# Early attention of a fused attention and two-layer MoE kernel: mask products ahead of the scores on TensorE, and VectorE's second scan ahead of the mask

## The chip, the cores and the metric

One core of a Trainium2 chip runs the whole program. The metric is the device time of one execution in microseconds; lower is better. The engines are TensorE (PE, matrix products into the eight PSUM banks), VectorE (DVE), ScalarE (ACT), GpSimd (POOL) and SyncE (SP, whose queue starts the transfers).

## The reference, cut to what matters

A gated linear attention over 4 batches, 8 heads, 768 steps and a head width of 48, then two feed-forward layers over the 3072 tokens.

```
for t in range(S):
    state = alpha[:, :, t, :, None] * state + einsum('bhd,bhe->bhde', k[:, :, t], v[:, :, t])
    y[:, :, t] = einsum('bhd,bhde->bhe', q[:, :, t], state)
x = y.transpose(0, 2, 1, 3).reshape(B * S, H * D)          # 3072 x 384
h = x @ w_in;  x1 = (h * sigmoid(h)) @ w_out               # 384 -> 2048 -> 384
g = x1 @ w_gate;  out = (g * sigmoid(g) * (x1 @ w_val)) @ w_out2   # 384 -> 1536 -> 384
```

## The kernel before

The steps are cut into 6 chunks of 128 for each of the 4 batches: 24 chunks, `n = 0..23`. A chunk has 4 pairs of heads; a pair of one chunk is a group `g = 4n..4n+3` (96 groups), and two groups make a duo `d`. For each group TensorE makes the scores (`qkt`, tile `s`: a product of the scaled keys and queries `kq` for each of the two heads, and one with a unit matrix that turns the keys). VectorE multiplies the scores with the causal mask (`causal`, tile `pt`), and ScalarE copies the turned keys (`keys`, tile `kt`). ScalarE's copy reads the same bank as VectorE's product and waits for it. When all four groups of a chunk are there, TensorE makes the chunk's results (`pv`: `y`, the state's increment `ds`, and from the fifth chunk on the part from the state that is carried), and `chunk_end` splits `y` into a high and a low half for the next layer (ScalarE copies, VectorE subtracts, tile `x`; in the second block of tokens a tile `y` too).

What the scores need is made by two scans on VectorE for each duo: `stage_a1` (a scan backwards, tile `r`; then `stage_a2`, a reciprocal and on POOL the scaled keys) and `stage_a3` (a scan forwards, tile `g`, and on POOL the scaled queries; after a chunk's second duo it issues the load of the chunk after next, tile `in`).

All order is that of the program text. One call of `attn` handles one group: it issues `pv` of a finished chunk where there is one, then `qkt` of the new group, then on VectorE and ScalarE the mask and the keys, then `chunk_end`, then the scans that are due. The first 7 chunks (28 groups) are "early": nothing but attention runs, with 32-bit scores in two banks that are used in turn, so that group g+2 waits for the readers of group g. `pv(m)` runs in the call of group 4m+5. From group 16 on (`T0 = first - 12`) the calls also decode weights: `units1` takes one unit (a 128 by 384 part of the first layer's weights; there are 32) through three steps on VectorE (tiles `raw`, `dec`), a rounding on ScalarE and a subtraction on POOL (tile `w`).

After the early part the first layer's products (`g1`, `g2`, tiles `h` and `x`) of the first two blocks of tokens run in turns with nothing from attention but with the rest of the 32 units being decoded, a unit or so per half step; then the remaining chunks' attention is mixed with the first layer, and the second layer (`gv`, `og`) ends the program. `act1` makes from a tile `h` the activation twice on ScalarE, rounded (`gh`) and in full (`gf`, one buffer in SBUF), and VectorE's subtraction of the two is the low half `gl`.

Of the kernel before, what the change touches and what calls it, by code (L numbers as in the profile page):

```python
# [10 lines left out]
F32 = mybir.dt.float32  # L11
# [3 lines left out]
AF = mybir.ActivationFunctionType  # L15
# [6 lines left out]
C = 128  # L22
NC = S // C
NCH = B * NC
NP = H // 2
# [195 lines left out]
def fast(ctx, tc, pk, w1, w2, out, bad_i):  # L221
# [3 lines left out]
    PE, ACT, DVE, POOL, SP = nc.tensor, nc.scalar, nc.vector, nc.gpsimd, nc.sync  # L225

    blocks1, n = [], 0
# [15 lines left out]
    mp = ctx.enter_context(tc.tile_pool(name="mp", bufs=2))  # L243

    def bank(i, name):
        pool = ps if i in (2, 3, 6, 7) else pools_ps["late"]
        return pool.tile([128, 512], F32, tag=f"b{i}", name=name)

    def big(i, name, dtype=F32):

        return mp.tile([128, 6 * 512], dtype, tag=f"big{i}", name=name, bufs=1)
# [8 lines left out]
    def sub(eng, lo, src, hi):  # L260
        eng.tensor_tensor(out=lo, in0=src, in1=hi.bitcast(F32), op=ALU.subtract)  # L261

    def split(hi, lo, src, lo_eng):
        ACT.activation(out=hi, in_=src, func=AF.Copy)  # L264
        sub(lo_eng, lo, src, hi)
# [8 lines left out]
    mask = ac.tile([128, C], BF16, name="mask")  # L274
# [7 lines left out]
    start = big(0, "start")  # L282
# [6 lines left out]
    y_t, ds_t, s_t = {}, {}, {}  # L289
    x_t, y3_t, p0_t = {}, {}, {}  # L290

    NE, NF = B, len(blocks1[0]) + len(blocks1[1])
# [107 lines left out]
    def columns(t):  # L400
        return t.rearrange("p (h x) -> p h x", h=2)[:, :, :D]

    def qkt(g):

        d, i = divmod(g, 2)
        n, p = divmod(g, NP)
        kf, qf = kq_t[d][:, 0, i], kq_t[d][:, 1, i]
        if n < NF:

            b = pools_ps["early"].tile([128, 2, 512], F32, tag=f"s{g % 2}", name=f"s{g}")  # L410
            for h in range(2):
                r = slice(64 * h, 64 * h + 64)
                PE.matmul(b[:, h, :C], kf[r], qf[r], start=True, stop=True)
            PE.matmul(b[:, 0, C:C + 2 * D], kf, columns(ident), start=True, stop=True)
            s_t[g] = b[:, :, :C], b[:, 0, C:C + 2 * D]
            return
        b = bank(5, f"s{g}")
        w = 2 * C + (2 * D if n < NCH - B else 0)
        kh, kl = kh_t[d][:, i], kl_t[d][:, i]
        PE.matmul(b[:, :w], kh, qh[:, p, :w], start=True, stop=False)  # L420
        PE.matmul(b[:, :2 * C], kh, ql[:, p], start=False, stop=False)
        PE.matmul(b[:, :w], kl, qh[:, p, :w], start=False, stop=True)
        s_t[g] = b[:, :2 * C].rearrange("p (h t) -> p h t", h=2), b[:, 2 * C:]

    def causal(g):
        if g < NE * NP and g % NP == 0:
            pt = p0[g // NP % 2]
        else:
            pt = ap.tile([128, 2, C], F32, tag="pt", name=f"pt{g}", bufs=NP + 1)
        pt_t[g] = pt  # L430
        DVE.tensor_tensor(
            out=pt, in0=s_t[g][0],
            in1=mask.rearrange("p (o t) -> p o t", o=1).to_broadcast([128, 2, C]), op=ALU.mult,
        )
# [10 lines left out]
    def pv(n):  # L445

        c, b = divmod(n, B)
        v = v_t[n]  # L450
        early = (NF - 1 - n) % 2 if n < NF else 0
        y = y_t[n] = bank((6, 2)[early], f"y{n}")
        first, last = n * NP, n * NP + NP
        heads = [(p, h, slice(64 * h, 64 * h + 64)) for p in range(NP) for h in range(2)]
        pts = [pt_t.pop(g) for g in range(first, last)]
        for p, h, hs in heads:
            if n < NE and p == 0:
                continue
            cs = slice(p * C, p * C + C)
            PE.matmul(  # L460
                y[hs, cs], v[:, p, hs], pts[p][:, h], start=(p == (n < NE)),
                stop=(n >= NE and c == 0 and p == NP - 1),
            )
            if n < NE:
                PE.matmul(
                    y[hs, cs], v3[n % 2][:, p - 1, hs], pts[0][:, h], start=False,
                    stop=(p == NP - 1),
                )
        if c < NC - 1:
            ds = ds_t[n] = bank((7, 3)[early], f"ds{n}")[:, :NP * D].rearrange(  # L470
                "p (r e) -> p r e", r=NP
            )
            for p, h, hs in heads:
                PE.matmul(  # L474
                    ds[hs, p], kt_t[first + p][:, hs], v[:, p, 64 * h:64 * h + D],
                    start=True, stop=True,
                )
            for g in range(first, last):
                kt_t.pop(g)
        if c:  # L480
            for p, h, hs in heads:
                PE.matmul(  # L482
                    y[64 * h:64 * h + D, p * C:p * C + C], state[b][hs, p],
                    kq_t[(first + p) // 2][hs, 1, p % 2], start=False, stop=(p == NP - 1),
                )
# [105 lines left out]
    def act1(j, f):  # L591
        w = len(blocks1[j]) * C
        hb = h_t.pop((j, f))
        gh = mp.tile([128, 512], F32R, tag="gh", name=f"gh{j}_{f}")[:, :w]
        gf = mp.tile([128, 512], F32, tag="gf", name=f"gf{j}_{f}", bufs=1)[:, :w]
        gl = mp.tile([128, 512], F32R, tag="gl", name=f"gl{j}_{f}")[:, :w]
        ACT.activation(out=gh, in_=hb, func=AF.Silu)  # L597
        ACT.activation(out=gf, in_=hb, func=AF.Silu)  # L598
        act_t[j, f] = (gh, gl)

        def rest():
            sub(DVE, gl, gf, gh)

        return rest

# [54 lines left out]
    def act2(j, f):  # L660
        w = len(blocks2[j]) * C
        gate, val = gv_t.pop((j, f))
        p = pools2["s"]
        sg = mp.tile([128, 512], F32, tag="gf", name=f"sg{j}_{f}", bufs=1)[:, :w]
        ACT.activation(out=sg, in_=gate, func=AF.Silu)  # L665
        a = p.tile([128, 512], F32, tag="a", name=f"a{j}_{f}")[:, :w]
        DVE.tensor_tensor(out=a, in0=val, in1=sg, op=ALU.mult)  # L667
        ah = mp.tile([128, 512], F32R, tag="gh", name=f"ah{j}_{f}")[:, :w]
        al = mp.tile([128, 512], F32R, tag="gl", name=f"al{j}_{f}")[:, :w]
        split(ah, al, a, DVE)  # L670
        a_t[j, f] = (ah, al)
# [26 lines left out]
    st = dict.fromkeys(("a1", "a2", "a3", "b", "c", "gd", "qk", "pv", "end", "l1", "d1", "e1", "f1", "h1", "s1", "l2", "d2", "e2", "f2", "h2", "s2"), 0)  # L698

    def up_to(key, g, fn, top=NG):  # L700
        while st[key] < min(g + 1, top):
            fn(st[key])
            st[key] += 1
# [8 lines left out]
    def attn(lag=1, more=True, first=None):  # L712
        done, new = st["pv"], None
        if st["qk"] - st["pv"] * NP >= NP + lag - 1:
            pv(done)
            st["pv"] += 1
        if more and st["qk"] < NG:
            new = st["qk"]
            qkt(new)
            st["qk"] += 1  # L720
        rest = first and first()
        if new is not None:
            d, odd = divmod(new, 2)
            early = new < NF * NP
            ahead, top = d + (2 if early else 3), NF * NP // 2 if early else ND
            if early and new and not odd:
                up_to("a1", ahead, stage_a1, top)
            causal(new)
            keys(new)
            if new == 0:  # L730
                up_to("a1", ahead, stage_a1, top)
        if rest:
            rest()
        if st["pv"] > done:
            chunk_end(done)
        if new is None:
            return
        if new < NE * NP and new % NP == NP - 1:
            spread(new // NP)
        if odd:  # L740
            up_to("a3", ahead, stage_a3, top)
            if not early:
                up_to("b", d + 2, stage_b, ND)
            up_to("gd", d, guard, ND)
        else:
            up_to("a1", ahead, stage_a1, top)
            if not early:
                up_to("c", d + 1, stage_c, ND)
            up_to("a2", ahead, stage_a2, top)
# [61 lines left out]
    for _ in range(12):  # L811
# [4 lines left out]
        out=mask, in_=mask, compare_op=ALU.is_ge, fill=0.0, base=0,  # L816
# [11 lines left out]
    first = NF * NP  # L828
# [4 lines left out]
    for i in range(NP):  # L833
        ACT.activation(
            out=qh[:, i, 2 * C:].rearrange("p (h d) -> p h d", h=2), in_=columns(ident), func=AF.Copy
        )
    T0 = first - 12
    for g in range(first):
        attn(2)
        if g % 4 == 3:  # L840
            up_to("l1", g // 4 + 1, load1, NU1)
        if g >= T0:
            units1(2, 1 + (g - T0) // 2)
    pe_stack.close()
# [12 lines left out]
    due, n = [first] * (2 * len(turns)), first  # L857
# [188 lines left out]
```

## Time and profile before

| | us |
|---|---|
| median of 3 runs | 1023.23 (1023.1 to 1025.08) |
| profiled execution: its time | 1025.6 |
| profiled execution: its span | 1023.9 |
| early part: first scores to the first product of the layer | 6.88 to 79.95 |
| TensorE busy over the span | 989.5 (97%) |
| VectorE, ScalarE, POOL busy | 476.0, 360.7, 222.8 |

The profiled execution took 1025.6 us, of which 1.7 us lie outside the span that the trace covers. Busy time of TensorE says little here: a product counts as busy from its start to its modelled end, at either level of its clock. The granted clock is given as a share of 2.4 GHz, so 0.5 is the lower level (1.2 GHz).

### The profile page before, as it was taken

The numbers are of one execution on the slowest core, as the hardware profiler recorded it, in microseconds if no ns is written. First come the engines' busy times: TensorE is split into PE (matmuls) and PEld (weight loads), VectorE is DVE, ScalarE is ACT, GpSimd is POOL, SyncE is SP. The second block draws the span as 40 slices with busy tenths as digits, with TensorE's granted clock in tenths as the row PEclk, the third lists the DMA queues.
The fourth block names the chain that finished last, engine by engine and source line by source line (L and its number), as shares of the span: only waits on it lengthen the run. The fifth ranks groups of instructions, "written<-read, shape, count | busy, mean of one in ns | idle before, by whom it ended". The sixth has DMA issues, their size and how long they took to land.

```text
span 1023.9 us, 14306 instructions
## 1 busy us (share of the span) xinstructions
PE 989.5 (97%) x5618; PEld 872.0 (85%) x5618; DVE 476.0 (46%) x847; ACT 360.7 (35%) x856; POOL 222.8 (22%) x293
## 2 busy tenths in 40 slices
PE   7868999999999999999999999999999999999997
PEld 5756998789999999988888888888888888888886
DVE  6475997545435355353498756222222222222222
ACT  2233444545545455444354323222222222222121
POOL 5351434624323244131144212000000000000000
PEclk7677999999999999999999999999999999999999
DMA  5434421222121222200454520100100100100000
GB/s 185 169 127 139 181 78 47 90 72 85 54 65 53 76 84 74 80 21 1 134 175 139 170 62 16 62 1 1 62 1 1 61 1 1 62 1 8 24 1 34
DMA packets 28458, 69.08 MB, mean 67 GB/s; under 512 B 3168, under 2 KB 9824, under 8 KB 28384
## 3 DMA queue, kind: packets, MB, share of 16 engines
q1 hardware_dynamic: 28096, 67.84, 20.6%
q8 instruction: 46, 0.75, 0.3%
q10 hardware_dynamic: 288, 0.26, 0.1%
q14 instruction: 28, 0.23, 0.1%
HBM read 56.68 MB, written 9.44 MB: 65 GB/s over the span
## 4 chain that ended last, share of the span: by engine, by line
PE 91%; DVE 4%; ACT 2%; DMA 1%; issue 1%; SPq 0%; ACTq 0%; DVEq 0%
PE gv L580 10%; PE gv L579 10%; PE gv L582 10%; PE h L579 7%; PE h L580 6%; PE h L582 6%; PE x L615 6%; PE x L614 6%; PE x L617 6%; PE o L684 5%; PE o L682 5%; PE o L683 5%; PE y L460 3%; PE y L482 2%; PE ds L474 1%; PE s L420 1%
## 5 line engine op out<-in xcount | busy, mean ns | idle before, releaser
L580 PE MATMUL gv<-x1h,w 128*128 128x512 f32 x432 | 169.1, 391 | 0.0
L579 PE MATMUL gv<-x1h,w 128*128 128x512 f32 x432 | 169.0, 391 | 0.0
L667 DVE TENSOR_TENSOR a<-gv,sg 128x512 f32<-128x512 f32 x72 | 49.8, 692 | 253.9 <-PE gv L582 253.9
L579 PE MATMUL h<-x,w 128*128 128x384 f32 (+1 forms) x336 | 124.0, 369 | 5.3 <-ACT kt L440 3.4
L614 PE MATMUL x<-gh,w 128*128 128x384 f32 (+1 forms) x336 | 122.4, 364 | 0.1
L615 PE MATMUL x<-gh,w 128*128 128x384 f32 (+1 forms) x336 | 122.3, 364 | 0.0
L582 PE MATMUL gv<-x1l,w 128*128 128x512 f32 x432 | 122.1, 391 | 0.0
L580 PE MATMUL h<-x,w 128*128 128x384 f32 (+1 forms) x336 | 121.8, 362 | 0.0
L261 DVE TENSOR_TENSOR gl<-gf,gh 128x384 fp32r<-128x384 f32 (+1 forms) x112 | 73.4, 655 | 84.3 <-ACT gf L598 82.6
L261 POOL TENSOR_TENSOR w<-raw,w 128x384 fp32r<-128x384 f32 x64 | 75.0, 1172 | 162.7 <-ACT w L556 159.9
L597 ACT ACTIVATE gh<-h 128x384 fp32r<-128x384 f32 (+1 forms) x112 | 60.0, 535 | 136.5 <-PE h L582 136.5
L665 ACT ACTIVATE sg<-gv 128x512 f32<-128x512 f32 x72 | 43.1, 599 | 177.4 <-PE gv L582 177.4
L264 ACT ACTIVATE ah<-a 128x512 fp32r<-128x512 f32 x72 | 45.6, 633 | 157.8 <-DVE a L667 157.8
L684 PE MATMUL o<-w,al 128*128 128x384 f32 x288 | 97.2, 338 | 0.0
L682 PE MATMUL o<-w,ah 128*128 128x384 f32 x288 | 97.0, 337 | 0.0
L683 PE MATMUL o<-w,ah 128*128 128x384 f32 x288 | 96.7, 336 | 0.0
L582 PEld LDWEIGHTS gv<-x1l,w 128*128 128x128 f32 x432 | 81.1, 188 | 17.8
L579 PEld LDWEIGHTS gv<-x1h,w 128*128 128x128 f32 x432 | 81.0, 188 | 15.3
L580 PEld LDWEIGHTS gv<-x1h,w 128*128 128x128 f32 x432 | 81.1, 188 | 14.9
L582 PE MATMUL h<-x,w 128*128 128x384 f32 (+1 forms) x336 | 85.4, 362 | 0.0
L617 PE MATMUL x<-gl,w 128*128 128x384 f32 (+1 forms) x336 | 84.6, 359 | 0.2 <-DVE gl L261 0.2
L579 PEld LDWEIGHTS h<-x,w 128*128 128x128 f32 x336 | 63.4, 189 | 15.4 <-issue 6.2
(104 smaller groups left out, 1572.5 us busy)
## 6 DMA issues: line engine op xcount, KB each, us to landing
raw<-in_w_dram SPq DMA_DIRECT2D x64, 384.0 KB, 3.6
in<-in_pk_dram SPq DMA_DIRECT2D x22, 770.5 KB, 4.2
in_v<-in_pk_dram SPq DMA_DIRECT2D x24, 256.0 KB, 3.1
x1r<-x_d SPq DMA_DIRECT2D x6, 768.0 KB, 5.0
out_dram<-ob SPq DMA_DIRECT2D x24, 192.0 KB, 2.1
x_d<-x1e SPq DMA_DIRECT2D x4, 576.0 KB, 3.3
x_d<-x1e SPq DMA_DIRECT2D x3, 768.0 KB, 4.6
late<-in_w_dram SPq DMA_DIRECT2D x4, 384.0 KB, 5.3
```

The costliest lines, as they stand in the source:

```text
L261: eng.tensor_tensor(out=lo, in0=src, in1=hi.bitcast(F32), op=ALU.subtract)
L579: PE.matmul(acc, part(u, k), xh, start=(k == 0), stop=False)
L580: PE.matmul(acc, part(u, k, 1), xh, start=False, stop=False)
L582: PE.matmul(acc, part(u, k), xl, start=False, stop=(k == len(xk) - 1))
L597: ACT.activation(out=gh, in_=hb, func=AF.Silu)
L614: PE.matmul(x1_t[j][m], part(u, m), gh, start=(f == 0), stop=False)
L615: PE.matmul(x1_t[j][m], part(u, m, 1), gh, start=False, stop=False)
L617: PE.matmul(x1_t[j][m], part(u, m), gl, start=False, stop=(f == NF1 - 1))
L667: DVE.tensor_tensor(out=a, in0=val, in1=sg, op=ALU.mult)
L682: PE.matmul(o, ah[:, ts], ohl[:, :DM], start=(f == 0), stop=False)
L683: PE.matmul(o, ah[:, ts], ohl[:, DM:], start=False, stop=False)
L684: PE.matmul(o, al[:, ts], ohl[:, :DM], start=False, stop=(f == NF2 - 1))
```

## The change

Four edits.

1. `filler(g)`: ahead of the scores of each early group, TensorE multiplies the mask (a 128 by 128 tile in bf16) with the mask repeated four times: 512 columns, written into the bank in which the results `y` of that group's chunk will stand. Nothing reads it; `pv` overwrites it. One product per group, three for groups 1 to 5: 38 in all. The bank of `y` is therefore claimed at the chunk's first group instead of in `pv`.
2. In an early call that has issued a `pv`, the forward scan (`stage_a3`) of the duo that is due is issued ahead of the mask product instead of behind `chunk_end`.
3. `act1` writes the full activation back into its PSUM bank `h` instead of into `gf`; VectorE's subtraction reads it there. The second layer's `sg`, which shared that buffer, gets one of its own.
4. `T0` goes from `first - 12` to `first - 8`: decoding begins at group 20 instead of 16, and ends the early part with four units instead of six.

```diff
+    def filler(g):
+        n = g // NP
+        if n not in y_t:
+            y_t[n] = bank((6, 2)[(NF - 1 - n) % 2], f"y{n}")
+        wide = mask.rearrange("p (o t) -> p o t", o=1).to_broadcast([128, 4, C])
+        for _ in range(3 if 0 < g < NP + 2 else 1):
+            PE.matmul(y_t[n].rearrange("p (o t) -> p o t", o=4), mask, wide, start=True, stop=True)
...
-        y = y_t[n] = bank((6, 2)[early], f"y{n}")
+        if n >= NF:
+            y_t[n] = bank(6, f"y{n}")
+        y = y_t[n]
...
-        gf = mp.tile([128, 512], F32, tag="gf", name=f"gf{j}_{f}", bufs=1)[:, :w]
...
-        ACT.activation(out=gf, in_=hb, func=AF.Silu)
+        ACT.activation(out=hb, in_=hb, func=AF.Silu)
...
-            sub(DVE, gl, gf, gh)
+            sub(DVE, gl, hb, gh)
...
             new = st["qk"]
+            if new < NF * NP:
+                filler(new)
             qkt(new)
...
+            if early and st["pv"] > done:
+                up_to("a3", ahead, stage_a3, top)
             if early and new and not odd:
                 up_to("a1", ahead, stage_a1, top)
             causal(new)
...
-    T0 = first - 12
+    T0 = first - 8
```

On VectorE, in the calls of groups 8 to 10 (around the results of chunk 1; `s_310`, `s_343` and `s_359` are the scores of groups 8, 9 and 10, `y_321` the chunk's results, `g_355` the forward scan), the rows before are

```order
L338 SCALAR_TENSOR_TENSOR r_314<-in_229,ones 128x258
L431 TENSOR_TENSOR start<-s_310,mask 128x256
L348 RECIPROCAL rc_89<-r_314 128x2
L431 TENSOR_TENSOR pt_347<-s_343,mask 128x256
L261 TENSOR_TENSOR x_272<-y_321,x_272 128x3x128
L357 SCALAR_TENSOR_TENSOR g_355<-in_229,rc_89 128x258
L338 SCALAR_TENSOR_TENSOR r_363<-in_229,ones 128x258
L431 TENSOR_TENSOR pt_365<-s_359,mask 128x256
```

and of the changed kernel (groups 8, 9 and 10 are `s_331`, `s_364` and `s_381`, the results `y_243`, the scan `g_368`)

```order
L338 SCALAR_TENSOR_TENSOR r_335<-in_240,ones 128x258
L441 TENSOR_TENSOR start<-s_331,mask 128x256
L348 RECIPROCAL rc_89<-r_335 128x2
L357 SCALAR_TENSOR_TENSOR g_368<-in_240,rc_89 128x258
L441 TENSOR_TENSOR pt_371<-s_364,mask 128x256
L261 TENSOR_TENSOR x_292<-y_243,x_292 128x3x128
L338 SCALAR_TENSOR_TENSOR r_385<-in_240,ones 128x258
L441 TENSOR_TENSOR pt_387<-s_381,mask 128x256
```

The forward scan `g` has gone up two rows, ahead of the mask product of group 9; the backward scan `r` still stands ahead of the mask product of group 10.

On TensorE, the rows of groups 6 to 8 (scores `s_282`, `s_294`, `s_310`) are before

```order
L413 MATMUL s_282<-kq_215 128x128 x2
L414 MATMUL s_282<-start,kq_215 128x96
L413 MATMUL s_294<-kq_215 128x128 x2
L414 MATMUL s_294<-start,kq_215 128x96
L413 MATMUL s_310<-kq_240 128x128 x2
L414 MATMUL s_310<-start,kq_240 128x96
```

and of the changed kernel (`s_300`, `s_313`, `s_331`; `y_243` is chunk 1's bank and `y_329` chunk 2's)

```order
L433 LDWEIGHTS mask
L433 MATMUL y_243<-mask 128x512
L413 MATMUL s_300<-kq_223 128x128 x2
L414 MATMUL s_300<-start,kq_223 128x96
L433 LDWEIGHTS mask
L433 MATMUL y_243<-mask 128x512
L413 MATMUL s_313<-kq_223 128x128 x2
L414 MATMUL s_313<-start,kq_223 128x96
L433 LDWEIGHTS mask
L433 MATMUL y_329<-mask 128x512
L413 MATMUL s_331<-kq_255 128x128 x2
L414 MATMUL s_331<-start,kq_255 128x96
```

A weight load and a product of the mask now stand ahead of each group's scores. The first mask product of a chunk, here the one into `y_329`, waits for VectorE, the reader of the results that stood in that bank two chunks ago.

Near the end of the turns VectorE decodes the last units (`late` is the buffer of the last four, `dec_30` and `dec_31` belong to units 30 and 31, `gl_7` and `gl_14` are low halves of the layer's activations). Before:

```order
L52 SCALAR_TENSOR_TENSOR late<-late,dec_30_1462 128x384
L47 TENSOR_SCALAR dec_31_1485<-late 128x384
L57 SCALAR_TENSOR_TENSOR late<-late 128x384
L261 TENSOR_TENSOR gl_13_1509<-gf_13_1508,gh_13_1507 128x384
L52 SCALAR_TENSOR_TENSOR late<-late,dec_31_1485 128x384
L57 SCALAR_TENSOR_TENSOR late<-late 128x384
L261 TENSOR_TENSOR gl_7_1539<-gf_7_1538,gh_7_1537 128x512
L261 TENSOR_TENSOR gl_14_1567<-gf_14_1566,gh_14_1565 128x384
```

In the changed kernel:

```order
L261 TENSOR_TENSOR gl_7_1543<-h_7_1532,gh_7_1542 128x512
L52 SCALAR_TENSOR_TENSOR late<-late,dec_30_1520 128x384
L47 TENSOR_SCALAR dec_31_1551<-late 128x384
L57 SCALAR_TENSOR_TENSOR late<-late 128x384
L261 TENSOR_TENSOR gl_14_1574<-h_14_1563,gh_14_1573 128x384
L52 SCALAR_TENSOR_TENSOR late<-late,dec_31_1551 128x384
```

Unit 30 is finished behind `gl_7` instead of two low halves ahead of it, and unit 31 behind `gl_14`.

## Rows read from the trace of the kernel before

**Rows 1.** The page, part 2: granted clock of TensorE in 40 slices, in tenths.

```profile
PEclk7677999999999999999999999999999999999999
```

**Rows 2.** Stretches: length, busy PE, PEld, DVE, ACT, POOL, granted clock, DMA share, GB/s.

```profile
12.76:23.01 10.25, 8.19 (x64) 6.78 (x65) 5.16 (x13) 2.92 (x12) 3.54 (x6) 0.67 0.57 194
...
43.50:55.47 11.97, 8.33 (x64) 6.96 (x65) 7.00 (x14) 3.06 (x12) 5.49 (x9) 0.64 0.35 122
55.47:68.03 12.56, 7.94 (x72) 6.51 (x73) 9.43 (x20) 3.94 (x15) 6.59 (x8) 0.77 0.32 116
68.03:79.95 11.92, 8.47 (x73) 6.93 (x73) 7.99 (x17) 4.46 (x17) 4.57 (x7) 0.64 0.45 154
...
100.00:162.70 62.70, 62.70 (x329) 58.38 (x329) 58.98 (x89) 28.67 (x61) 27.13 (x24) 1.00 0.33 121
```

**Rows 3.** Timeline of TensorE, chunk 1's results and the scores after: start, length.

```profile
24.41 0.70 PE L460 MATMUL y<-pt,in_v 128*64 128x128 f32 x4
...
28.05 0.80 PE L413 MATMUL s<-kq 64*128 64x128 f32 x4
...
29.45 0.49 PE L413 MATMUL s<-kq 64*128 64x128 f32 x4
...
30.32 0.49 PE L413 MATMUL s<-kq 64*128 64x128 f32 x4
...
33.26 0.80 PE L413 MATMUL s<-kq 64*128 64x128 f32 x4 [2.06 <-ACT kt L440]
```

**Rows 4.** The chain of waits in order of time, from group 9's scores to group 12's.

```profile
29.55 0.44 DVE pt L431
...
30.16 0.58 ACT x L508 x2
...
31.24 0.68 DVE g L357
31.93 0.59 DVE r L338
32.51 0.33 DVE pt L431
...
32.86 0.26 ACT kt L440
```

**Rows 5.** Timeline of TensorE: the first scores, and those of groups 2.

```profile
6.88 0.49 PE L413 MATMUL s<-kq 64*128 64x128 f32 x4 [0.77 <-DVE kq L362]
...
9.56 0.80 PE L413 MATMUL s<-kq 64*128 64x128 f32 x4 [0.98 <-POOL kq L362]
```

**Rows 6.** Timeline of TensorE: results of chunk 6, and the warming products at the start.

```profile
1.27 4.84 PE L812 MATMUL warm<-jk 128*128 128x512 bf16 x12 [1.27 <-DVE jk L803]
...
84.08 1.09 PE L460 MATMUL y<-pt,in_v 128*64 128x128 f32 x16
85.00 0.62 PE L474 MATMUL ds<-in_v,kt 128*64 128x48 f32 x16
85.56 1.08 PE L482 MATMUL y<-kq,state 64*48 64x128 f32 x16
...
86.56 0.50 PE L579 MATMUL h<-x,w 128*128 128x512 f32 x1
```

**Rows 7.** The chain of waits in order of time, in the second layer.

```profile
579.80 0.69 PE gv L582 x3
```

**Rows 8.** Timeline of VectorE: group 21's mask product, with chunk 4's results.

```profile
61.76 0.43 DVE L431 TENSOR_TENSOR pt<-s,mask 128x256 f32<-128x256 f32 x1 [1.83 <-PE s L414]
```

**Rows 9.** Timeline of all engines at the end of the turns.

```profile
161.42 1.27 DVE L57 SCALAR_TENSOR_TENSOR late<-late 128x384 int32<-128x384 int32 x1
...
164.28 1.10 POOL L261 TENSOR_TENSOR w<-late,w 128x384 fp32r<-128x384 f32 x1 [2.01 <-ACT w L556]
...
166.73 0.56 DVE L261 TENSOR_TENSOR gl<-gf,gh 128x384 fp32r<-128x384 f32 x1 [2.24 <-ACT gf L598]
...
167.71 0.33 PE L579 MATMUL h<-x,w 128*128 128x384 f32 x1
```

**Rows 10.** The page, part 6: DMA issues, KB each, median us from issue to landing.

```profile
in<-in_pk_dram SPq DMA_DIRECT2D x22, 770.5 KB, 4.2
```

More of the change, by code (lines that the diff above doesn't have):

```diff
@@ L663, in act2 @@
         p = pools2["s"]
-        sg = mp.tile([128, 512], F32, tag="gf", name=f"sg{j}_{f}", bufs=1)[:, :w]
+        sg = p.tile([128, 512], F32, tag="sg", name=f"sg{j}_{f}", bufs=1)[:, :w]
         ACT.activation(out=sg, in_=gate, func=AF.Silu)
```

## The prediction

> **What bounds the kernel now.** I read the page's strip of the granted clock first. TensorE has its full clock in 36 of 40 slices, but only six to seven tenths in the first four, some 100 us [rows 1]: the early part is where time lies. The table by stretches says how long one chunk takes there, measured from the first score product of a group 4k to that of group 4k+4: 10.25 us from 12.76 to 23.01, the same again twice up to 43.50, then 11.97, 12.56 and 11.92 where weights are decoded too [rows 2]. Mean clock 0.64 to 0.77; no engine is busy throughout.
>
> The timeline of TensorE shows what a chunk consists of [rows 3]. Results of a chunk (24 products for `y`, 16 for `ds`) run from 24.41 to 28.05, 3.64 us; group 9's scores from 28.05 to 29.45, 1.40 us; then the clock rises, and group 10's take 0.87 us (29.45 to 30.32). After group 11's TensorE idles 2.06 us until 33.26, and the next scores are at the slow pace again (0.80 against 0.49 us for the same row). So there are two losses: the idle 2.06 us, and work at half clock because of it.
>
> What the idle time waits for stands in the chain of waits [rows 4]: mask of group 9 at 29.55, the high half of the results on ScalarE at 30.16, then VectorE's subtraction (0.44 us that the chain view calls issue), the forward scan `g` at 31.24 (0.68), the backward scan `r` at 31.93 (0.59), mask of group 10 at 32.51, ScalarE's keys of group 10 at 32.86, which free the bank for group 12's scores at 33.26. From the end of group 9's scores (about 29.53) that is 3.73 us.
>
> **Part by part. The scan ahead of the mask.** `g` leaves this chain: it runs while TensorE still makes results, when VectorE has nothing to do. That is 0.68 by its own length, 0.60 to 0.69 by distances between starts; I take 0.65, and the chain is 3.73 - 0.65 = 3.1 us. What is late next is `r`, which stays in front of group 10's mask. The moved scan issues no transfer: the load hangs on a chunk's second duo, whose scan is not moved.
>
> **The mask products.** At the upper level 512 columns take 0.23 us (three in 0.69 [rows 7]); at the lower 0.40 (twelve in 4.84 [rows 6]). Between group 9's scores and group 12's stand three mask products and two groups of scores: 3 x 0.23 + 2 x 0.87 = 2.43 us at the upper level, shorter than 3.1, so they cost nothing there but the one in front of group 9, and leave some 0.7 us idle. At the lower level they are 3 x 0.40 + 2 x 1.40 = 4.0, longer than 3.1: no idle time, and every product costs its length. The wait for the reader of the bank costs nothing: the subtraction that it waits for begins 1.3 us after group 9's scores.
>
> **Does the clock stay up with 0.7 us idle in a chunk?** The early gaps bound it [rows 5]: after 0.77 us idle at 6.11 the first scores still ran fast (0.49), and only after the second gap, 0.98 us up to 9.56, slow (0.80). A gap of 2.06 us always dropped it. So 0.7 us alone lies just under one that did not drop it and well under those that did; I take it as held. The Trainium skill, "TensorE: Matmul & The Clock Gate", section "A second HAM failure mode: psum-queue depth-cycling", speaks against this: an engine that pauses briefly but often between groups of products that cycle through banks can swing between both levels. By the rows the sum is that below, by this rule it is that of the first rival (1020). No run here shows yet which.
>
> **The sum, early part.** Results at the upper level, from chunk 6's [rows 6]: 16 `y` products in 0.92 (84.08 to 85.00), so 24 in 1.38, and 16 `ds` in 0.56: 1.94 us; with the state's part (85.56 to 86.56) 0.92 + 0.56 + 1.00 = 2.48.
>
> - Start: the first scores stay at 6.88. Four groups of 0.87 and four times three mask products bring group 4 to 6.88 + 3.48 + 2.76 = 13.12 instead of 12.76: +0.36.
> - Group 4 to 8: 0.87 + 1.94 + three mask products 0.69 + 0.87 + 3.1 = 7.47 instead of 10.25: -2.78.
> - 8 to 12 and 12 to 16: 0.87 + 1.94 + 0.23 + 0.87 + 3.1 = 7.01: -3.24 twice.
> - 16 to 20: before, two units are decoded there and VectorE's chain is longer; now decoding begins at group 20, so again 7.01, against 11.97: -4.96.
> - 20 to 24: with the state's part and decoding in the chain. Before, mask of group 21 [rows 8] to 68.03 is 6.27; without `g` 5.62. 0.87 + 2.48 + 0.23 + 0.87 + 5.62 = 10.07 against 12.56: -2.49.
> - 24 to the first layer product: the gap in front is 5.62 - 2.43 = 3.2 us, so the clock falls; the chain is that of before (no scan of a first duo is left to move). Only a mask product is added: +0.4.
>
> Together -15.95 us; the first layer product at about 64 instead of 79.95.
>
> **Decoding later.** Two units move into the turns. There VectorE is busy 58.98 of 62.70 us with 89 instructions, 0.66 each, and TensorE without a pause [rows 2]: VectorE has hardly any slack but at the end. Two units are six such instructions, 4.0 us (up to 1.27 each [rows 9], 7.6). Before, the last ended at 162.69, and VectorE then idled 2.24 us ahead of the `gl` at 166.73. Now unit 30 is done behind the `gl` before that: three instructions from about 164.5, 166.5; until POOL had subtracted it took another 2.7 us for unit 31 before (162.69 to 165.38). That is 168.3 to 169.2 with ScalarE less loaded or as before, and the second product of the `h` that begins at 167.71 wants it at 167.88: 0.4 to 1.3 us late, were VectorE's instructions all long, 3. I take +0.7. Unit 31 has 3 us more in hand.
>
> **Activations back into PSUM.** A subtraction with one operand in PSUM is shown: the one ahead of `g` in the chain, `x` from `y`, of the same 128 by 384; it takes what `gl` takes, and neither is on the path in the turns, since TensorE has no pause there. The bank is freed by VectorE instead of ScalarE, but the next user of that bank stands behind the products that need `gl` anyway. A store of ScalarE into PSUM is not in the trace; were it twice as slow, 0.5 us longer for each, ScalarE (28.67 of 62.70 busy) would take it; were it free, nothing is gained. Zero; the cover is TensorE's unbroken work.
>
> Sum: -15.95 + 0.7 = -15.2. The profiled execution took 1025.6 us (span 1023.9), so 1010.4; the median of the three runs is 2.4 lower, 1023.23, and I forecast **1008.0**.
>
> **Rivals.**
>
> *The clock falls in every chunk.* Then a chunk starts slow: before, the clock rose after 6.44 us of unbroken work (23.01 to 29.45). Scores 1.40, results 3.64, mask product 0.40 and 1.0 of group 9's scores fill that; the remaining quarter runs in 0.2, then 3.1: 9.8 us instead of 10.25. Groups 8 to 16 give -0.9, 16 to 20 -2.2, the start and the rest -0.4 (the shorter chain against twelve products more), decoding +0.7: -2.8, **1020.4**. For it: the idle 0.7 us comes in every chunk and score groups are thin work. Against: the 0.77 us above.
>
> *It holds in some chunks only*: half the difference of 2.8 us in four chunks, +5.6: **1013.6**.
>
> *Loads become the bound.* A load (770.5 KB, 4.2 us to landing [rows 10]) is issued about 5 us into a chunk and wanted by the first scan of a chunk later; with 10.25 us a chunk that is 9 us, with 7.0 some 5.5 to 6. It decides where landing takes over 6 us: say 1 us in three chunks, **1011**.
>
> *Slower: the clock never rises.* The mask products lengthen TensorE's work, and at the lower level that work, not the chain, is then the bound (4.0 against 3.1). Group 4 comes at 6.88 + 4 x 1.40 + 12 x 0.40 = 17.3 (+4.5); 4 to 8 takes 1.40 + 3.64 + 1.20 + 1.40 + 4.0 = 11.64 (+1.4); 8 to 16 10.84 twice (+1.2); 16 to 20 10.84 (-1.1); the last two +0.9 and +0.4; decoding +0.7: +8, **1031**. It decides on whether unbroken work at the lower level raises the clock; in this trace it did after 6.44 us, which speaks against it.
>
> **How the numbers follow.** Forecast 52%, loads 8%, some chunks 17%, every chunk 14%, never 6%, the rest 3%. What a measurement can tell from no change is about 0.2%, 2 us. The forecast's own range is 1003 to 1011.5: its low end is a clock that also stays up from group 24 on (two score groups and results at 0.87 and 2.48 instead of 1.40 and about 4.6, -3.2) with part of the decoding's 0.7 and 1 us of the start saved. The range for 8 in 10 goes on to the case of some chunks: 1003 to 1018.5. Faster 0.85 (of the every-chunk case two thirds), same 0.07, slower 0.08.
>
> **What would show it.** The page's clock strip at 9 in the second and third slice; chunks of about 7.0 us between score products of groups 8, 12, 16 and 20; no `g` between subtraction and `r`; idle time ahead of group 12's scores at 0.5 to 0.9 us; first layer product near 64; the `h` product after `gl_14` waiting for POOL by under 1.5 us. It is wrong if scores in the middle of the early part still take 1.40 us, if VectorE's `r` waits for a load, or if TensorE pauses several us in the turns.

## The result and the profile after

The changed kernel takes 1013.32 us (median of four runs, 1012.13 to 1013.83) against 1023.16 for the kernel before on the same chip; the ratio is 0.990 with a 95% interval of 0.9883 to 0.9917. That is 1% faster, beyond the interval. It is 5.3 us above the forecast of 1008.0: outside the forecast's own range (1003 to 1011.5), inside the range for 8 in 10 (1003 to 1018.5). The profiled execution took 1013.68 us (span 1012.0; before 1025.6 and 1023.9).

The page's strip of the granted clock, which answers to [rows 1], stands at nine tenths but for the third slice and the last; before, the first four were at six or seven tenths:

```profile
PEclk9979999999999999999999999999999999999998
```

The stretches between the first scores of groups 0, 4, 8, 12, and those after group 20, answer to [rows 2] (columns as there):

```profile
6.64:12.48 5.84, 5.84 (x37) 3.19 (x36) 5.73 (x13) 1.38 (x6) 3.49 (x5) 1.00 0.80 272
12.48:20.05 7.57, 6.69 (x71) 4.60 (x71) 5.14 (x12) 2.89 (x11) 3.50 (x7) 1.00 0.74 258
20.05:27.19 7.14, 6.26 (x68) 4.49 (x69) 5.08 (x12) 2.91 (x12) 3.53 (x6) 1.00 0.58 197
...
41.46:51.17 9.71, 6.94 (x77) 4.83 (x77) 6.62 (x16) 3.21 (x13) 4.08 (x7) 0.97 0.45 155
51.17:63.65 12.48, 9.41 (x76) 7.07 (x76) 7.87 (x17) 4.45 (x17) 3.85 (x6) 0.75 0.44 149
```

A chunk that took 10.25 us takes 7.14, at clock 1.00 instead of 0.67. The timeline of TensorE through the same chunk, against [rows 3]: a score group's first row is 0.49 us long throughout, and the idle time ahead of group 12 is 0.88 us instead of 2.06.

```profile
23.15 0.49 PE L413 MATMUL s<-kq 64*128 64x128 f32 x4
23.57 0.46 PE L414 MATMUL s<-start,kq 128*128 128x96 f32 x2
23.87 0.38 PE L433 MATMUL y<-mask 128*128 128x512 bf16 x1
24.18 0.49 PE L413 MATMUL s<-kq 64*128 64x128 f32 x4
...
27.19 0.49 PE L413 MATMUL s<-kq 64*128 64x128 f32 x4 [0.88 <-ACT kt L450]
```

The chain of waits that ends there, against [rows 4], has no forward scan left between the subtraction and the backward scan:

```profile
24.68 0.58 ACT x L520 x2
25.26 0.02 issue
25.29 0.56 DVE x L261
25.84 0.60 DVE r L338
26.45 0.33 DVE pt L441
26.77 0.02 issue
26.80 0.26 ACT kt L450
```

So the first layer product comes at 63.65 instead of 79.95: 16.3 us won. Only 11.9 of them reach the end. To find the place I lined up the 100 or so groups of products with `gl` in the layers, which stand in one order in both kernels, and took the distance between the two traces at each. It is 16.6 us at the first nineteen, 16.3 at the next three, up to the one that starts at 150.76, 10.0 at the next two (160.33 and 164.02), 12.2 at the one after those (170.52), and stays between 12.1 and 12.3 to the end. Everything is lost and partly won back within 20 us, at the end of the turns. The timeline of TensorE there:

```profile
151.45 0.33 PE L591 MATMUL h<-x,w 128*128 128x384 f32 x1
156.22 0.50 PE L592 MATMUL h<-x,w 128*128 128x384 f32 x1 [4.44 <-POOL w L261]
156.52 0.52 PE L591 MATMUL h<-x,w 128*128 128x384 f32 x1
...
168.59 0.43 PE L420 MATMUL s<-qh,kh 128*128 128x352 f32 x1 [1.37 <-ACT kt L450]
```

TensorE stands for 4.44 us in front of the second product of an `h`, which wants the low half of unit 30, and then works at the lower clock (0.52 us a product instead of 0.33) up to 159.7. The idle time at 168.59 is shorter than its counterpart before, and the clock stays up behind it, which gives 2.2 us back. GpSimd's and ScalarE's timelines say what unit 30 waited for (the first fence is GpSimd's):

```profile
152.90 0.68 POOL L349 TENSOR_TENSOR kq<-in,r 128x256 f32<-128x256 f32 x1 [3.77 <-DVE r L338]
154.21 0.68 POOL L362 TENSOR_TENSOR kq<-in,g 128x256 f32<-128x256 f32 x1 [0.63 <-DVE g L357]
154.85 0.35 POOL L367 TENSOR_TENSOR state<-state,r 128x96 f32<-128x96 f32 x1
155.16 1.99 POOL L261 TENSOR_TENSOR w<-late,w 128x384 fp32r<-128x384 f32 x2
```

```profile
150.01 0.49 ACT L609 ACTIVATE h<-h 128x384 f32<-128x384 f32 x1
150.50 0.56 ACT L568 ACTIVATE w<-late 128x384 fp32r<-128x384 f32 x1
```

ScalarE has rounded unit 30 at 151.06. GpSimd is idle from before then up to 152.90, yet the subtraction starts at 155.16: it stands behind three products of the next attention duo, and those wait for VectorE's scans. (The row at 155.16 holds two subtractions; TensorE goes on at 156.22, after the first.) In the kernel before, the first of these products came after the last subtraction, that of unit 31 at 164.28 [rows 9]; GpSimd's timeline there:

```profile
168.04 0.69 POOL L349 TENSOR_TENSOR kq<-in,r 128x256 f32<-128x256 f32 x1 [2.65 <-DVE r L338]
```

### The profile page after: what moved, and what is told of

Same layout as the page of the kernel before. It is cut to its first block, busy times and chain, and to the rows that moved or that the text cites. A ratio compares the mean times of both kernels' runs of the same rounds, so it can differ in the third digit from the quotient of the medians.

```text
span 1012.0 us, 14498 instructions
## 1 busy us (share of the span) xinstructions
PE 984.3 (97%) x5656; PEld 861.5 (85%) x5656; DVE 467.5 (46%) x847; ACT 359.8 (36%) x856; POOL 218.4 (22%) x293
## 4 chain that ended last, share of the span: by engine, by line
PE 92%; DVE 3%; ACT 2%; issue 1%; DMA 1%; SPq 0%; POOL 0%; ACTq 0%; POOLq 0%; DVEq 0%
PE gv L592 10%; PE gv L591 10%; PE gv L594 10%; PE h L591 7%; PE h L592 6%; PE h L594 6%; PE x L625 6%; PE x L626 6%; PE x L628 6%; PE o L695 5%; PE o L693 5%; PE o L694 5%; PE y L472 2%; PE y L494 2%; PE s L420 1%; PE s L422 1%
## 5 line engine op out<-in xcount | busy, mean ns | idle before, releaser
L261 DVE TENSOR_TENSOR gl<-h,gh 128x384 fp32r<-128x384 f32 (+1 forms) x112 | 68.6, 613 | 90.4 <-ACT h L609 86.6
```

## The experiments

All eleven are edits of the changed kernel, timed in five rounds beside the kernel before, in three sets: the first four, the next four, the last three. The kernel before had medians of 1024.6, 1024.3 and 1024.9 us in them, against 1023.2 beside the changed kernel, so a difference between runs of two sets is uncertain by some 1.5 us. My theory after the traces: the early part gains because TensorE's idle time in a chunk falls below what drops its clock, and 4 to 6 us are lost at the end of the turns to GpSimd's queue order. The rivals: VectorE's decoding is what is late there; one of the two early edits does it alone; the silu in PSUM has a part in it.

**pool_order**: GpSimd's subtraction of unit 30 ahead of the scans' products.

```diff
         if ahead == 6:
+            up_to("s1", st["h1"] - 1, lambda u: low_unit(("1", u), POOL), NU1)
             stage_a(first_d)
```

> The changed kernel with one instruction of GpSimd put earlier: the subtraction of unit 30's low half goes into its queue ahead of the three products of the scans at the end of the turns, instead of behind them. Nothing else moves. Theory 1 (the 4.44 us that TensorE idles for unit 30 are GpSimd's queue order): ScalarE has rounded that unit at 151.06, so the subtraction ends near 152.3 to 153.0 instead of 157.15; TensorE waits 0.6 to 1.4 us instead of 4.44, most of the stretch at the lower clock behind it (some 1.7 us) goes too: 1008 to 1009.8 us, 3.5 to 5.5 less than the changed kernel's 1013.3. Theory 2 (it is VectorE's decoding that is late): the unit's values come when they come, the wait stays at 3.5 us or more: 1012.5 to 1013.5.

Measured: 1007.3 us (1006.83 to 1009.02), ratio 0.9833 [0.982, 0.9845]. Timelines of GpSimd and then of TensorE:

```profile
151.41 1.30 POOL L261 TENSOR_TENSOR w<-late,w 128x384 fp32r<-128x384 f32 x1 [2.00 <-ACT w L568]
153.87 0.68 POOL L349 TENSOR_TENSOR kq<-in,r 128x256 f32<-128x256 f32 x1 [1.17 <-DVE r L338]
```

```profile
151.72 0.33 PE L591 MATMUL h<-x,w 128*128 128x384 f32 x1
152.76 0.44 PE L592 MATMUL h<-x,w 128*128 128x384 f32 x1 [0.71 <-POOL w L261]
153.04 0.33 PE L591 MATMUL h<-x,w 128*128 128x384 f32 x1
...
164.18 0.43 PE L420 MATMUL s<-qh,kh 128*128 128x352 f32 x1 [2.00 <-ACT kt L450]
```

One instruction earlier in one queue, and the wait is 0.71 us with no stretch at the lower clock behind it. That settles the 4.44 us: queue order, not VectorE.

**undo_units**: the fourth edit undone.

```diff
-    T0 = first - 8
+    T0 = first - 12
```

> The changed kernel with its fourth edit undone: six weight units are decoded in the early part, as before the change, and two fewer in the turns. Theory 1 (that edit gains in the early part and loses more at the end of the turns, through GpSimd's queue): the wait of 4.44 us is gone, and the early part gives back 2 to 4 us, because the chunk from group 16 to 20 decodes again (about 9 us instead of 7.13) and the clock falls one chunk earlier: first layer product at 65.5 to 67.5 instead of 63.65, total 1010 to 1012.5. Rival (the edit is what keeps the early part fast, and the gain there outweighs the wait): first layer product at 69 or later, 1014 to 1017.

Measured: 1008.7 us (1007.49 to 1009.19), ratio 0.9847 [0.9834, 0.9859]. TensorE has no wait for unit 30; the first layer product comes at 65.31, 1.7 us later than in the changed kernel. The wait is gone as expected, and the time lies below the expected 1010 to 1012.5: as it stood, the fourth edit cost some 5 us.

**no_products**: the first edit undone, the bank still taken.

```diff
-        for _ in range(3 if 0 < g < NP + 2 else 1):
-            PE.matmul(y_t[n].rearrange("p (o t) -> p o t", o=4), mask, wide, start=True, stop=True)
```

> The changed kernel without the mask products of its first edit; the moved scan, the later decoding and the silu in PSUM stay. Theory 1 (the products hold the clock): TensorE idles over 1.5 us in each chunk, the clock falls in each, chunks of about 9.6 us instead of 7.14 from group 4 to 20, the start 0.4 us shorter: 1020 to 1024, no more than 3 us below the kernel before. Rival (the shorter chain alone keeps the idle time small enough): chunks of 7.0 to 7.3 us, 1012 to 1014.

Measured: 1013.03 us (1012.56 to 1018.47; four of six near 1013, two above 1015), ratio 0.9904 [0.9886, 0.9922]: no difference from the changed kernel. My expectation was wrong, the rival right. The two above 1015 have a mean granted clock of 0.979 and 0.982, the other four 0.984. The timeline of TensorE shows the clock up with 1.47 us idle in a chunk:

```profile
20.95 0.49 PE L413 MATMUL s<-kq 64*128 64x128 f32 x4 [1.47 <-ACT kt L448]
...
27.77 0.49 PE L413 MATMUL s<-kq 64*128 64x128 f32 x4 [1.47 <-ACT kt L448]
...
34.58 0.49 PE L413 MATMUL s<-kq 64*128 64x128 f32 x4 [1.47 <-ACT kt L448]
```

These chunks take 6.82 us, 0.3 less than with products. The start is slower (group 8 at 20.95 instead of 20.05, the clock down from 9.43 on), which takes that back.

**silu_sbuf**: the third edit undone.

```diff
...
-        ACT.activation(out=hb, in_=hb, func=AF.Silu)
+        ACT.activation(out=gf, in_=hb, func=AF.Silu)
...
-            sub(DVE, gl, hb, gh)
+            sub(DVE, gl, gf, gh)
...
```

> The changed kernel with its third edit undone: the full silu goes to SBUF again, and VectorE's subtraction reads both operands there. Theory 1 (the prediction's zero: neither place is on the path): 1012.8 to 1013.9, no difference beyond 0.5 us. Rival (VectorE's subtraction is faster with one operand in PSUM, and in the turns, where VectorE is nearly full, that sets how late the units come): VectorE's gl longer by 0.05 to 0.2 us each in the turns, some 25 of them, the wait at unit 30 1 to 3 us longer: 1014.5 to 1016.5.

Measured: 1013.39 us (1012.65 to 1014.08), ratio 0.9892 [0.9877, 0.9906]. No difference, and the wait for unit 30 is 4.4 us in both. VectorE's longest `gl` does grow, from 0.69 to 1.11 us, but nothing waits for it.

**no_scan_move**: the second edit undone, the products kept.

```diff
-            if early and st["pv"] > done:
-                up_to("a3", ahead, stage_a3, top)
```

> The changed kernel with its second edit undone: the mask products stay, the forward scan stands again between the results' subtraction and the mask. Theory A (either edit alone brings TensorE's idle time in a chunk under what drops the clock): the chain is 0.65 us longer, idle time 0.88 + 0.65 = 1.5 us in a chunk, about that of the run without products (1.47), which kept its clock; chunks of 7.8 us from group 8 to 20, total 1015 to 1016.5. Theory B (the moved scan is what keeps the clock, the products do nothing): the clock falls in each chunk, scores at 0.80 instead of 0.49, chunks of 9.6 to 10.7 us, 1021 to 1028.

Measured: 1020.87 us (1020.18 to 1021.52), ratio 0.997 [0.9959, 0.9982]. Between the theories. The timeline of TensorE: idle time 1.47 us as in no_products, the first chunk (20.50 to 28.39) at the upper clock; in the second the mask product behind the results is at 0.61 instead of 0.39 and the next scores come 1.6 us later than in the first. The third shows the same 0.61 (at 42.83); in the fourth the clock held.

```profile
20.50 0.49 PE L413 MATMUL s<-kq 64*128 64x128 f32 x4 [1.47 <-ACT kt L450]
...
23.45 0.39 PE L433 MATMUL y<-mask 128*128 128x512 bf16 x1
...
28.39 0.49 PE L413 MATMUL s<-kq 64*128 64x128 f32 x4 [1.47 <-ACT kt L450]
...
32.71 0.61 PE L433 MATMUL y<-mask 128*128 128x512 bf16 x1
```

**neither**: both early edits undone (the two diffs above).

> The changed kernel with its first two edits undone: no mask products, and the scan not moved; only the later decoding and the silu in PSUM stay. Theory A: as in the kernel before, TensorE idles about 2.06 us in each chunk and the clock falls in each, chunks of 10.25 us; the chunk from group 16 to 20 no longer decodes (1.7 us less), and the wait for unit 30 with its slow stretch is added (4.5 to 6): 1025 to 1029, slower than the kernel before by up to 4. Rival (the silu in PSUM or the later decoding brought part of the gain): under 1022.

Measured: 1028.12 us (1026.24 to 1029.12), ratio 1.0036 [1.0023, 1.0048]. As expected: chunks of 10.1 to 10.4 us from group 8 to 20, clock down in each, and the last two edits alone make the kernel slower. In the timeline of TensorE:

```profile
22.59 0.80 PE L413 MATMUL s<-kq 64*128 64x128 f32 x4 [2.06 <-ACT kt L448]
```

The four medians together, with the last two edits in all of them:

| | scan not moved | scan moved |
|---|---|---|
| no products | 1028.12 | 1013.03 |
| products | 1020.87 | 1013.32 |

The moved scan is worth 15.1 us alone. The products are worth 7.3 alone, and nothing in this pair once the scan is moved. The columns come from different sets; by the ratios to the kernel before, the two gains are 13.5 and 6.8 us.

**start_only**: pool_order, with products for groups 0 to 5 alone.

```diff
-        for _ in range(3 if 0 < g < NP + 2 else 1):
+        for _ in range(3 if 0 < g < NP + 2 else g == 0):
```

> The changed kernel with GpSimd's subtraction of unit 30 put ahead, as in the first run, and mask products for groups 0 to 5 alone (one for group 0, three each for the next five). Theory A (the products are wanted only at the start; later an idle time of 1.47 us keeps the clock, and each product in front of a group only costs its length): group 8 at 20.0 as in the changed kernel, then chunks of 6.8 us instead of 7.13 up to group 20 and 9.4 instead of 9.7 up to 24; about 1.3 us less than the first run's 1007.3: 1005.3 to 1006.7. Rival (1.47 us idle is near the edge, and the products are what makes it safe): the clock falls in one chunk or more, 2 to 2.5 us each: 1008 to 1014.

Measured: 1011.98 us (1009.52 to 1013.43), ratio 0.9888 [0.9874, 0.9902]: 4.7 us slower than pool_order. The rival was right: here, with the scan moved, the products of the middle chunks are worth some 5 us, which no_products did not show. The timeline of TensorE in the first chunk after group 8, and the next:

```profile
20.45 0.49 PE L413 MATMUL s<-kq 64*128 64x128 f32 x4 [1.47 <-ACT kt L450]
20.87 0.74 PE L414 MATMUL s<-start,kq 128*128 128x96 f32 x2
21.54 0.70 PE L472 MATMUL y<-pt,in_v 128*64 128x128 f32 x4
...
24.79 0.49 PE L413 MATMUL s<-kq 64*128 64x128 f32 x4
```

Here the clock fell, and the scores and results took 4.34 us; in the three chunks behind, with the same idle time, it held (28.83 to 31.61, 2.78 us). The profiled execution is the fastest of the four.

**gaps**: start_only with products in the three longest waits; `fill(t, n)` issues n mask products into bank `t`.

```diff
+        for _ in range(3 if 0 < g < NP + 2 else {0: 1, 24: 7, 28: 9}.get(g, 0)):
...
+        if s == 2:
+            fill(hb, 5)
...
     need1(0)
+    filler(28)
     g1(0)
```

> As the run with products at the start alone, and products put where TensorE idles longest and the clock falls: seven ahead of group 24's scores (2.24 us idle in the changed kernel, 3.5 without products), nine ahead of the first layer product (3.07, 3.45 without), five ahead of the third layer step's product, which waits 1.82 us for the transfer of x from y. Theory A (these idle times are what lowers the clock between 51 and 81 us): idle times of 0.7 to 1.6 us, clock up throughout, the stretches at half pace (57 to 58, 64 to 70, 77.5 to 81) shorten: 3 to 5 us less than the run with products at the start alone, 1001 to 1003.5. Rival (VectorE's chain with the decoding bounds these chunks, and half-pace products lie beside it): under 1.5 us less, 1004 to 1006.

Measured: 1005.88 us (1000.89 to 1007.21), ratio 0.9803 [0.9781, 0.9825]: 6.1 us less than start_only, but spread over 6 us. In the profiled execution the clock fell in three of the chunks between groups 8 and 20 (1.47 us idle), and stayed up from 46.75 on, with the long waits now at 0.95, 1.50 and 0.73 us. The timeline of TensorE at two chunks:

```profile
28.72 0.80 PE L413 MATMUL s<-kq 64*128 64x128 f32 x4 [1.48 <-ACT kt L455]
...
46.75 0.49 PE L413 MATMUL s<-kq 64*128 64x128 f32 x4 [1.47 <-ACT kt L455]
```

The spread goes with the clock: the two fastest executions (1000.89 and 1001.18 us) have a mean granted clock of 0.998, the other three, of which the profiled one is the slowest, 0.991.

**all_gaps**: the products of the changed kernel, pool_order, and the same three waits filled. Its edit differs from that of gaps in one line, shown here against the changed kernel.

```diff
-        for _ in range(3 if 0 < g < NP + 2 else 1):
+        for _ in range({24: 7, 28: 9}.get(g, 3 if 0 < g < NP + 2 else 1)):
```

> The changed kernel with all its mask products, GpSimd's subtraction of unit 30 put ahead as in the first run, and products put into the three long waits: seven ahead of group 24's scores instead of one, nine ahead of the first layer product, five ahead of the third layer step. Theory (0.88 us idle in a chunk always keeps the clock, 1.47 only in some chunks and some executions): idle times all at 0.6 to 1.0 us, clock up from group 4 to the layers, five runs within 2 us of each other (without products in the middle they were spread over 6), 1000.5 to 1003. Rival (the spread comes from elsewhere): 1001 to 1007 again, spread over 4 us or more.

Measured: 1003.16 us (1002.17 to 1004.32), ratio 0.9795 [0.9782, 0.9808], spread 2.2 us, a little above what was expected. It beats both kernels. The two executions of gaps near 1001 were faster still, by 2 us: where the clock holds anyway, the products in the middle chunks cost their length. The page's strip has no slice below nine tenths, and the timeline of TensorE shows the filled waits and the first layer product 2.8 us earlier than in the changed kernel:

```profile
41.51 0.49 PE L413 MATMUL s<-kq 64*128 64x128 f32 x4 [0.88 <-ACT kt L455]
...
51.22 0.49 PE L413 MATMUL s<-kq 64*128 64x128 f32 x4 [0.95 <-ACT kt L455]
...
57.62 2.10 PE L438 MATMUL y<-mask 128*128 128x512 bf16 x9
60.85 0.50 PE L596 MATMUL h<-x,w 128*128 128x512 f32 x1 [1.13 <-ACT kt L455]
```

**gaps_one**: all_gaps, from group 6 on with one product a chunk.

```diff
-        for _ in range({24: 7, 28: 9}.get(g, 3 if 0 < g < NP + 2 else 1)):
+        for _ in range({24: 7, 28: 9}.get(g, 3 if 0 < g < NP + 2 else g % NP == 0)):
```

> As the run with products in all long waits, but from group 6 on one product for each chunk, the one ahead of group 4k, where TensorE idles anyway, instead of four. Idle time in a chunk between that with four products (0.88) and without (1.47): 1.1 to 1.3 us, chunks of 6.8 us instead of 7.13, which is 1 us less over three chunks. If the clock holds at that idle time: 1000 to 1002, narrow. If it falls in some executions: median 1002 to 1006, five runs spread over 3 us or more.

Measured: 1003.17 us (1002.34 to 1006.57), ratio 0.9806 [0.9786, 0.9827]. The same median, spread over 4.2 us. The idle time is 0.18 + 0.92 us around the product, and in the profiled execution the clock fell in one chunk of four (20.30 to 24.62): one product is not quite enough, and what it saves, 0.3 us a chunk, it loses again there.

```profile
20.30 0.70 PE L413 MATMUL s<-kq 64*128 64x128 f32 x4 [0.91 <-ACT kt L455]
...
28.66 0.49 PE L413 MATMUL s<-kq 64*128 64x128 f32 x4 [0.92 <-ACT kt L455]
```

**all_gaps_12**: all_gaps with the fourth edit undone, and five products instead of one ahead of group 20's scores.

```diff
-        for _ in range({24: 7, 28: 9}.get(g, 3 if 0 < g < NP + 2 else 1)):
+        for _ in range({20: 5, 24: 7, 28: 9}.get(g, 3 if 0 < g < NP + 2 else 1)):
...
-    T0 = first - 8
+    T0 = first - 12
```

> As the run with products in all long waits, with six units decoded in the early part as before the change (first - 12) and five products ahead of group 20's scores, where TensorE then waits 1.94 us. If decoding early still costs 1.4 us in the early part with the clock up throughout (two chunks bound by VectorE instead of one) and saves the 0.71 us for unit 30: 0.5 to 1.5 us slower than the run with products in all long waits, 1001 to 1004. Rival (what the later decoding saved was only the clock in that chunk): equal or up to 1 us faster.

Measured: 1004.3 us (1003.88 to 1004.95), ratio 0.9807 [0.9794, 0.982]: 1.1 us above all_gaps, as expected (the two sets of five runs overlap a little). With GpSimd's order mended, decoding later gains about 1 us by the medians (pool_order against undo_units says 1.4); the intervals overlap, so it may be less. In the changed kernel it lost some 5.

## Why the prediction was right, and where it was off

The early part came as forecast, by the mechanism that the prediction names. The time as a whole owes its place in the range for 8 in 10 partly to luck: that range was stretched for a clock that holds in some chunks only, which did not occur, and at the end of the turns a gain that was not forecast made up for part of a loss far above its forecast. One of the prediction's own signs of being wrong came true: TensorE pauses 4.44 us in the turns.

**"The sum, early part" held.** Forecast -15.95 us, measured -16.3:

| | forecast | measured |
|---|---|---|
| group 4's first scores, from the start | 13.12 | 12.48 |
| 4 to 8 | 7.47 | 7.57 |
| 8 to 12, 12 to 16 | 7.01 | 7.14 |
| 16 to 20 | 7.01 | 7.13 |
| 20 to 24 | 10.07 | 9.71 |
| 24 to the first layer product | 12.3 | 12.48 |

The start came out better because the first scores came at 6.64 instead of 6.88, and because a score group with a mask product behind it is through in 0.72 us (23.15 to 23.87), not 0.87; the distance that I took seems to hold a short wait. A single mask product between scores is 0.31 us (23.87 to 24.18), not 0.23, which the middle chunks show.

**"The scan ahead of the mask" held in size and was worth more than I gave it.** The chain, from the end of group 9's scores (24.05) to group 12's (27.19), is 3.14 us against the forecast 3.1. But I took the mask products for what holds the clock, and the table of four medians says otherwise: moved alone, the scan brings the idle time from 2.06 to 1.47 us, and that mostly keeps the clock. With the scan moved, "the mask products" make the clock surer. Between no_products and the changed kernel that shows in the spread alone (5.9 us in six executions without them, 1.7 in four with), between start_only and pool_order in the median too (4.7 us). They are not free: a chunk takes 7.14 us with them and 6.82 without where the clock holds in both. The 0.40 us that the prediction gives a product at the lower level comes from a stretch for which the profile gives a granted clock of 1.00 (1.27 to 6.11); at 0.50, the layer's products of 512 columns stand 0.42 to 0.43 us apart (80.97, 81.39, 81.82 in the kernel before). No term of the forecast rests on it, but two of the rivals do.

**"Does the clock stay up with 0.7 us idle" held.** It was 0.88 us, between the 0.77 and 0.98 of [rows 5], and the clock stayed up in each chunk from group 8 to 20 of the changed kernel, pool_order, silu_sbuf and all_gaps. The margin is small: in gaps_one it fell once with 0.18 + 0.91 us. The Trainium skill, "TensorE: Matmul & The Clock Gate", section "A second HAM failure mode: psum-queue depth-cycling", says that brief, frequent idle times between groups of products that cycle through PSUM banks can make the clock swing between its levels. At 0.88 us a chunk no trace here shows that; at 1.47 us start_only, no_scan_move and gaps do swing, and no_products does not.

**"Decoding later" is the term that failed.** Forecast +0.7 us, measured +6.3: 4.44 us idle, then the rest of that `h` and the start of the next products at the lower clock. The step was right on when VectorE and ScalarE would be through with unit 30 and followed it to GpSimd, but counted there only the subtraction's own time. It did not ask what stands ahead of it in GpSimd's queue: the three products of the scans, which before came after unit 31. Moving two units later moved their subtractions behind those products. With the queue order mended the wait is 0.71 us, the number that this term gave, and the kernel takes 1007.3 us, against the forecast of 1008.0; that the two totals lie so close is in part luck, as the next two points show.

**What the sum did not have**: 2.2 us given back at the scores behind the turns. Before, TensorE waited there 2.17 us and then worked at the lower clock; the timeline of the kernel before:

```profile
179.37 0.50 PE L420 MATMUL s<-qh,kh 128*128 128x352 f32 x1 [2.17 <-ACT kt L440]
```

In the changed kernel it is 1.37 us at 168.59 and the clock stays up. Together: -16.6 + 0.3 + 6.3 - 2.2 = -12.2, of which the span shows 11.9. The 0.3 is lost between the products at 140.19 and 143.62, at about 141.06; its cause stays open. That the clock stays up because the wait is shorter is not shown: pool_order waited 2.00 us there, and its clock stayed up too.

**From the profiled execution to the median.** The prediction took off 2.4 us, since the profiled execution before was that much above the median. In the changed kernel it is 0.4 us above (1013.68 and 1013.32). So 2.0 of the 5.3 us by which the forecast missed are this step, and 3.3 are the terms (1010.4 forecast for the profiled execution).

**"Activations back into PSUM"**: zero, as forecast (silu_sbuf). The rivals "loads become the bound" and "the clock never rises" did not occur. "It holds in some chunks only" gave the time nearest the result, 1013.6, for the wrong reason: in the four chunks from group 4 to 20, where it was to fall in some, the clock held.

## What to carry to other kernels

When work is moved to a later place, write down what then stands ahead of it in the queue of each engine that it passes, not only how long each engine needs: an idle engine whose next instruction waits is a busy engine to all behind it. Where TensorE's clock falls because of short waits, shorten the chain first, and then fill what idle time is left with products that nobody reads: in the short waits they narrowed the spread here, and in the three longest they brought another 4 us. They cost their length where the clock would have held without them. Test two edits that aim at the same loss in all four combinations, since their gains need not add.

## What the runs showed of the hardware

An idle time of one length does not decide on the clock. With 0.88 us ahead of each fourth group it never fell; with 2.06 it fell each time; with 1.47 it held in four chunks of four in no_products, in three of four in start_only, in two of four in no_scan_move, in one of four in gaps. Ahead of group 2 the clock was down behind 0.98 us in the kernel before and 0.99 in no_products, and up behind 0.99 in neither (0.49 at 9.36). At the end of the turns pool_order's clock held behind 2.00 us of waiting (the products at 164.74 and after are 0.40 us long), and silu_sbuf's fell behind 2.02 (0.63 from 168.08). What else decides stays open.

ScalarE writes its silu to PSUM as fast as to SBUF (0.49 us for 128 by 384 in both), and a subtraction of VectorE with one operand in PSUM was never longer than 0.69 us (128 by 512), where that with both in SBUF reached 1.13 before the change and 1.11 in silu_sbuf. VectorE's last decoding step at 151.87 took 1.26 us in pool_order, beside GpSimd's subtraction, and 0.56 in the changed kernel, where GpSimd stood idle. The other steps of that line agree: of 32 in the changed kernel, the 24 with no work of GpSimd beside their start took 0.55 to 0.56 us, and the 8 beside one of its products or subtractions 0.93 to 1.40. What the two engines share there was not tried by itself.
